# The second softmax's transposes in six of eight batches: 32x32 blocks on VectorE and 16 DMAs in place of TensorE's transposes

## The chip, the cores and the metric

The kernel runs on one core of one Trainium2 chip. The metric is the device time of one execution in microseconds (us). A profiled execution also has a span: the time from its first to its last recorded instruction.

## The reference

An attention of 8 batches between 512 tokens and 32 state rows per head (8 heads of 64), in both directions, feeds a dense feed-forward layer and a layer of 8 experts with one expert per token. The change touches the second direction only (`scores2`, `a2`, `sread`).

```
scores = scale * np.matmul(x, state.transpose(0, 1, 3, 2))
...
xread = np.matmul(a, state)
scores2 = scale * np.matmul(state, x.transpose(0, 1, 3, 2))
scores2 = scores2 - scores2.max(-1, keepdims=True)
a2 = np.exp(scores2)
a2 /= a2.sum(-1, keepdims=True) + 1e-09
sread = np.matmul(a2, x)
return np.concatenate([xread, sread], axis=2)
...
h = x @ w_in
g = h * np.clip(h + 3.0, 0.0, 6.0) / 6.0
x = g @ w_out
# then: logits, argmax over 8 experts, relu(x @ w1[e]) @ w2[e], two gates
```

## The kernel before

A batch's dense layer is a segment of 16 steps, one for each 128 of the 2048 hidden columns. In a step TensorE makes the hidden block `h` (`h_xread`, L470, 6 matmuls of 128x512), ScalarE and VectorE turn it into a high part `gh` and a low part `gl` (`act`, L499 to L502), and two steps later TensorE multiplies them into four output banks (`gemm2`, L509 to L511, 12 matmuls). So a step is 18 matmuls of equal shape.

In between stands the attention of the next batch, started by hand at numbered steps (`timetable`). `attn_rows` computes the scores once, with both softmaxes' inputs in two PSUM banks (tag `misc`); `columns` takes the exponentials for the second softmax into two tiles `e2` of 128x512. A row of such a tile is one state row of one head (four heads, 32 rows each), a column is a token. `cols_turn` (step 6) transposes them by TensorE in eight pieces of 128x128 into two `misc` banks (L378), and ScalarE copies them into two tiles `a2T` (L374), with tokens on the partitions. `cols_read` (step 7) multiplies `a2T` with the tokens `xq` in 32 small matmuls (L393, two passes each) and ScalarE scales the result (L399); `cols_x1` (step 8) transposes that result (L421) and keeps it in `x1h` and `x1l` for the last segment. `one_run` keeps the matmuls of such a part together and gives its first one every wait of the part.

Batch 0 and batch 1 are handled by a plan written out by hand (`plan`, `attn_cols`), batch 2 by `half_timetable`, batches 3 to 7 by `timetable`. Their `cols_turn` comes at 75, 128, 174, 210, 285, 361, 436 and 512 us in the profile.

The Tile scheduler orders each engine's instructions within what the program allows. Each engine then runs its list in order. All loads and most stores are issued by the SP queue, also in order; a DMA takes one of eight semaphores in turn, and the one that comes eight later waits until it has landed. The tag `x4` has four buffers of 512 KB: per batch two halves of the transposed tokens (`xT`) and two halves of the tokens (`xq`), and early on the raw weights and the two tiles `part`.

Of the kernel before, what the change touches and what calls it, by code (L numbers as in the profile page):

```python
# [8 lines left out]
F32 = mybir.dt.float32  # L9
# [4 lines left out]
ALU = mybir.AluOpType  # L14
# [4 lines left out]
NB, NH, NQ, NS, HD = 8, 8, 512, 32, 64  # L19
# [60 lines left out]
def tile_kernel(  # L80
# [16 lines left out]
    V, S, G, T, D = nc.vector, nc.scalar, nc.gpsimd, nc.tensor, nc.sync  # L97
# [3 lines left out]
    def pool(c, name, bufs=1, side=None, space=None):  # L101
        kw = {"space": space} if space else {}
        return c.enter_context(tc.tile_pool(name=name, bufs=bufs, side=side, reuse_waits="tile", **kw))
# [6 lines left out]
    ap = pool(actx, "ap", 2, side="right")  # L110
# [34 lines left out]
    def not_yet(i):  # L145

        tc.add_manual_dep(i.ins, marks[-1].name, LATER, reason="has time")
# [9 lines left out]
    st_t, aT, loads, e2_t, x_in, q_in = {}, {}, {}, {}, {}, {}  # L157
# [27 lines left out]
    def misc():  # L185
        users.append([])
        return psum("misc", 2), users[-1]

    def one_run(*parts):

        behind = [i for u in users[-2:] for i in u]
        built = [p() for p in parts]
        first = None
        for mms, needs, _ in built:
            behind += needs
        for mms, _, _ in built:
            for m in mms:
                i = m().ins
                if first is not None:
                    tc.add_manual_dep(i, first.name, LATER, reason="all at once")  # L200
                    continue
                first = i
                for d in behind:
                    tc.add_manual_dep(first, d.name, DEP, reason="banks are free and all operands are there")
        for b in built:
            b[2]()
# [139 lines left out]
    def columns(b, src, done=None):  # L346

        e2, sm = e2_t[b]
        mx, nm, s2, r2 = [sm[:, 2 * k:2 * k + 2] for k in range(4)]
        e2_t[b] = e2, s2, r2, []  # L350
        for e in range(2):
            i = V.tensor_reduce(mx[:, e:e + 1], src[e], axis=AX.X, op=ALU.max)
            if b < 2:
                not_yet(i)
            V.tensor_scalar(nm[:, e:e + 1], mx[:, e:e + 1], -0.125, None, op0=ALU.mult)
            j = S.activation(e2[e], src[e], AF.Exp, bias=nm[:, e:e + 1], scale=0.125, accum_out=s2[:, e:e + 1])
            e2_t[b][3].append(j.ins)
            if done:
                done[e] += [i.ins, j.ins]

    def cols_turn(b):

        e2, s2, r2, exps = e2_t.pop(b)
        V.tensor_scalar(s2, s2, 1e-9, None, op0=ALU.add)
        V.reciprocal(r2, s2)

        def part():
            made = [misc() for _ in range(2)]
            a2 = [ap.tile([128, 4, 128], F32, tag="wy", name="a2T", bufs=2) for _ in range(2)]

            def use():
                copies = []
                for e in range(2):
                    copies.append(S.copy(a2[e].rearrange("p a n -> p (a n)"), made[e][0]).ins)  # L374
                    made[e][1].append(copies[-1])
                e2_t[b] = a2, r2, copies

            return [lambda e=e, i=i: T.transpose(made[e][0][:, 128 * i:128 * i + 128],  # L378
                                                 e2[e][:, 128 * i:128 * i + 128], ident)
                    for e in range(2) for i in range(4)], exps, use  # L380

        return part

    def cols_read(b):

        def part():
            a2, r2, copies = e2_t[b]
            x_q = [loads.pop((b, k, "q")) for k in range(2)]
            psR, done = misc()

            def mm(e, i, j):
                h = 2 * j + e
                return T.matmul(psR[32 * j:32 * j + 32, HD * e:HD * e + HD], a2[e][:, i, 32 * j:32 * j + 32],  # L393
                                x_q[h // 4][:, i, HD * (h % 4):HD * (h % 4) + HD], start=(i == 0), stop=(i == 3),
                                tile_position=(0, 32 * j))

            def use():
                for e in range(2):
                    done.append(S.activation(a2[0][:, 0, HD * e:HD * e + HD], psR[:, HD * e:HD * e + HD], AF.Copy,  # L399
                                             scale=r2[:, e:e + 1]).ins)  # L400
                e2_t[b] = a2[0][:, 0, :], list(done)

            return [lambda e=e, i=i, j=j: mm(e, i, j) for e in range(2) for i in range(4) for j in range(4)], \
                [*copies, *q_in[b]], use

        return part

    def cols_x1(b):

        def part():  # L410
            read, reads = e2_t.pop(b)
            psX, done = misc()
            psX = psX[:, :128]

            def use():
                hi, lo = [x[:, :, NS * b:NS * b + NS] for x in (x1h, x1l)]
                src = psX.rearrange("p (j s) -> p j s", j=4)
                done.append(V.tensor_copy(hi, src).ins)
                done.append(V.tensor_tensor(lo, src, hi.bitcast(F32), op=ALU.subtract).ins)

            return [lambda: T.transpose(psX, read, ident)], reads, use  # L421

        return part

    def attn_cols(b):

        if b < 2:
            columns(b, e2_t[b][0])
            yield
        one_run(cols_turn(b))  # L430
        yield
        one_run(cols_read(b))
        yield
        one_run(cols_x1(b))
        yield
# [116 lines left out]
    def write_rows(r, c):  # L552

        xr = mp.tile([128, 8, 128], F32, tag="xr", name="xr", bufs=2)
        for k in range(4):
            i = V.transpose(xr[:, :, 32 * k:32 * k + 32], r.x2[k][:, 256 * c:256 * c + 256])
            for d in r.made[1::2]:
                tc.add_manual_dep(i.ins, d.name, LATER, reason="banks first")
        r0 = 128 * r.tile0 + 256 * c
        rows = xd[r0:r0 + 256, :].rearrange("(a u) (g n) -> g u a n", u=32, g=4)  # L560
        for g in range(4):
            D.dma_start(rows[g], xr[32 * g:32 * g + 32])

    def logits(r):

        def part():
            psl, done = misc()

            def mm(k):
                return T.matmul(psl[32 * k:32 * k + 32, :r.n], wg_sb[:, k, :], r.x2[k], start=True, stop=True,  # L570
                                tile_position=(0, 32 * k))

            def use():
                r.l4 = mp.tile([128, 512], F32, tag="r", name="l4")[:, :r.n]
                done.append(S.copy(r.l4, psl[:, :r.n]).ins)
                r.l4_made = done[-1]

            return [lambda k=k: mm(k) for k in range(4)], list(r.made), use

        return part  # L580
# [74 lines left out]
    def read_rows(r, c):  # L655

        nt = min(2, r.nt - 2 * c)
        r0 = 128 * r.tile0 + 256 * c
        t = mp.tile([128, 2, DM], F32, tag="xr", name="xt", bufs=2)[:, :nt, :]
        G.dma_start(t, xd[r0:r0 + 128 * nt, :].rearrange("(t p) n -> p t n", p=128))  # L660
        r.rows.extend(t[:, k, :] for k in range(nt))
# [538 lines left out]
    def timetable(b, r, att, shift):  # L1200

        rows = attn_rows(b) if att else iter(())
        todo = {}

        def at(k, *fs):
            todo.setdefault(k, []).extend(fs)

        at(2 + shift, lambda: write_rows(r, 0))
        at(3 + shift, lambda: write_rows(r, 1))
        at(5 + shift, lambda: read_rows(r, 0))  # L1210
        at(6 + shift, lambda: read_rows(r, 1))
        for k in range(4, 10):
            at(k, lambda: next(rows, None))
        if att:
            at(6, lambda: one_run(cols_turn(b)))
            at(7, lambda: one_run(cols_read(b), logits(r)))
            at(8, lambda: one_run(cols_x1(b), turn_logits(r)))
        else:
            at(6, lambda: one_run(logits(r)))
            at(7, lambda: one_run(turn_logits(r)))  # L1220
        at(9, lambda: choose(r))
        at(10, lambda: ranks(r))
        at(11, lambda: place(r), lambda: sort_rows(r, 0, 2))
        at(12, lambda: sort_rows(r, 2, 4, marks[-1:]))
        at(13, lambda: scatter(r, marks[-1:]))
        return todo
# [236 lines left out]
```

## Time and profile before

| | |
|---|---|
| time, median of 3 runs | 1101.79 us (1101.53 to 1102.30) |
| the profiled execution: time, span | 1100.96 us, 1099.2 us |
| TensorE busy, share of the span | 1073.2 us, 98% |
| VectorE, ScalarE, GpSimd busy | 65%, 50%, 11% |
| granted TensorE clock, mean | 0.999 of full speed |

The profiled execution took 1.8 us more than its span and 0.8 us less than the median. TensorE (PE in the rows) is busy almost all the time; PEld are its weight loads, which overlap its matmuls, DVE is VectorE, ACT is ScalarE, POOL is GpSimd, SPq is the issuing SP queue. A matmul's row lasts longer than its distance to the next, since matmuls are pipelined: distances between starts tell what a piece costs.

### The profile page before, as it was taken

The numbers are of one execution on the slowest core, as the hardware profiler recorded it, in microseconds if no ns is written. First come the engines' busy times: TensorE is split into PE (matmuls) and PEld (weight loads), VectorE is DVE, ScalarE is ACT, GpSimd is POOL, SyncE is SP. The second block draws the span as 40 slices with busy tenths as digits, with TensorE's granted clock in tenths as the row PEclk, the third lists the DMA queues.
The fourth block names the chain that finished last, engine by engine and source line by source line (L and its number), as shares of the span: only waits on it lengthen the run. The fifth ranks groups of instructions, "written<-read, shape, count | busy, mean of one in ns | idle before, by whom it ended". The sixth has DMA issues, their size and how long they took to land. (4 is left out here: it accounts for less than half of the span.)

```text
span 1099.2 us, 18698 instructions
## 1 busy us (share of the span) xinstructions
PE 1073.2 (98%) x6748; PEld 845.6 (77%) x6748; DVE 714.5 (65%) x1518; ACT 553.7 (50%) x1058; POOL 126.2 (11%) x138
## 2 busy tenths in 40 slices
PE   4999999999999999999999999999999999999997
PEld 1577777777777777777777899888869887988994
DVE  7988676755746747556554486986646655667761
ACT  4979644433433434334333344565545654566651
POOL 0000001230030030110300311220010010001001
PEclk9999999999999999999999999999999999999999
DMA  7657043613214114211130159676486679922500
GB/s 252 213 168 248 16 138 96 172 45 77 78 41 116 41 39 116 70 36 53 39 77 1 39 148 288 131 255 231 148 305 186 240 230 334 340 64 64 177 21 31
DMA packets 81251, 147.38 MB, mean 134 GB/s; under 512 B 13232, under 2 KB 49840, under 8 KB 81136
## 3 DMA queue, kind: packets, MB, share of 16 engines
q1 hardware_dynamic: 71776, 118.03, 34.7%
q0 software_dynamic: 9376, 28.09, 7.4%
q8 instruction: 55, 0.90, 0.4%
q14 instruction: 44, 0.36, 0.1%
HBM read 146.05 MB, written 29.68 MB: 160 GB/s over the span
## 5 line engine op out<-in xcount | busy, mean ns | idle before, releaser
L509 PE MATMUL o<-gh,wo 128*128 128x512 f32 x512 | 202.8, 396 | 0.0
L510 PE MATMUL o<-gh,wo 128*128 128x512 f32 x512 | 200.2, 391 | 0.2 <-DVE wo L782 0.2
L511 PE MATMUL o<-gl,wo 128*128 128x512 f32 x512 | 200.1, 391 | 0.0
L500 DVE SCALAR_TENSOR_TENSOR g<-r,h 128x512 f32<-128x512 f32 x128 | 87.3, 683 | 115.1 <-ACT r L499 114.6
L499 ACT ACTIVATE r<-h 128x512 f32<-128x512 f32 x128 | 76.4, 597 | 158.0 <-PE h L470 157.8
L1044 DVE TENSOR_TENSOR vl<-w2s,vh 128x512 fp32r<-128x512 f32 x128 | 87.8, 690 | 63.8 <-ACT vh L1043 56.2
L501 ACT CAST gh<-g 128x512 fp32r<-128x512 f32 x128 | 79.4, 620 | 82.2 <-DVE g L500 81.2
L1043 ACT CAST vh<-w2s 128x512 fp32r<-128x512 f32 x128 | 78.9, 621 | 78.7 <-PE o L1060 72.1
L502 DVE TENSOR_TENSOR gl<-g,gh 128x512 fp32r<-128x512 f32 x128 | 88.2, 689 | 44.7 <-ACT gh L501 39.3
L509 PEld LDWEIGHTS o<-gh,wo 128*128 128x128 f32 x512 | 96.1, 188 | 26.4 <-issue 6.1
L510 PEld LDWEIGHTS o<-gh,wo 128*128 128x128 f32 x512 | 96.2, 188 | 22.5 <-issue 1.5
L511 PEld LDWEIGHTS o<-gl,wo 128*128 128x128 f32 x512 | 96.1, 188 | 21.5 <-issue 1.0
L1034 DVE TENSOR_TENSOR wl<-w1s,wh 128x512 fp32r<-128x512 f32 x128 | 87.1, 688 | 35.2 <-ACT wh L1034 24.8
L1060 PE MATMUL o<-vh,hl 128*128 128x512 f32 x256 | 100.3, 392 | 0.9 <-DVE hl L1048 0.9
L1059 PE MATMUL o<-vl,hh 128*128 128x512 f32 x256 | 100.2, 392 | 0.0
L470 PE MATMUL h<-ah,sh 128*128 128x512 f32 x240 | 99.1, 414 | 0.9 <-ACT sh L453 0.7
L470 PE MATMUL h<-al,sh 128*128 128x512 f32 x240 | 94.7, 395 | 0.1
L470 PE MATMUL h<-ah,sl 128*128 128x512 f32 x240 | 93.8, 392 | 0.0
L1034 ACT CAST wh<-w1s 128x512 fp32r<-128x512 f32 x128 | 78.0, 621 | 29.5 <-PE h L1038 27.9
L1038 PEld LDWEIGHTS h<-xh,wh 128*128 128x128 f32 x512 | 76.9, 188 | 14.8 <-DVE hl L1048 2.4
L1038 PE MATMUL h<-xh,wh 128*128 128x256 f32 x512 | 82.1, 282 | 1.8 <-DVE hl L1048 1.8
L1056 PE MATMUL o<-vh,hh 128*128 128x512 f32 x256 | 81.2, 398 | 0.0
(234 smaller groups left out, 1770.8 us busy)
## 6 DMA issues: line engine op xcount, KB each, us to landing
w1s<-w SPq DMA_DIRECT2D x88, 512.0 KB
w2s<-w SPq DMA_DIRECT2D x88, 512.0 KB
xd<-xr SPq DMA_DIRECT2D x68, 128.0 KB
xt<-xd POOLq DMA_DIRECT2D x17, 512.0 KB
xT<-xT SPq DMA_DIRECT2D x16, 512.0 KB
wi<-w_in SPq DMA_DIRECT2D x16, 512.0 KB
wraw<-w_out SPq DMA_DIRECT2D x16, 512.0 KB
xq<-xq SPq DMA_DIRECT2D x16, 512.0 KB
```

The source lines that it names most:

```text
L470: T.matmul(ps, w[:, o:o + 128], a[:, e, :], start=(n == 0), stop=(n == 5))
L500: V.scalar_tensor_tensor(g6, r, 6.0, ps, op0=ALU.min, op1=ALU.mult)
L502: V.tensor_tensor(gl, g6, gh.bitcast(F32), op=ALU.subtract)
L509: T.matmul(po[k][:, :n], woh[ft][:, s], gh, start=first, stop=False)
L510: T.matmul(po[k][:, :n], wol[ft][:, s], gh, start=False, stop=False)
L511: T.matmul(po[k][:, :n], woh[ft][:, s], gl, start=False, stop=last)
L1034: last_w[:] = [S.copy(wh, a).ins, V.tensor_tensor(wl, a, wh.bitcast(F32), op=ALU.subtract).ins]
L1038: T.matmul(ps, w[:, k, :], x[:, k, :], start=(m == 0), stop=(m == 11))
L1044: V.tensor_tensor(vl, c, vh.bitcast(F32), op=ALU.subtract)
L1056: T.matmul(py[t], hh[:, sl], vh, start=(ft == 0), stop=False)
L1059: T.matmul(py[t], hh[:, sl], vl, start=False, stop=False)
L1060: T.matmul(py[t], hl[:, sl], vh, start=False, stop=(ft == 7))
```

## The change

For batch 1 and batches 3 to 7 the eight transposes by TensorE, their two `misc` banks and ScalarE's two copies go. `cols_move`, at step 5, lets VectorE transpose all 32x32 blocks of the two `e2` tiles into one tile `e2t` (two instructions), and the SP queue then moves the 4 x 4 groups of blocks to their partitions with 16 DMAs of 32 partitions x 1 KB, into one tile `a2T` for both halves. `cols_read` picks its weights from the new layout; its matmuls are the same in number and shape. `e2t` and `a2T` are in the tag `x4`. Batches 0 and 2 stay as they were.

```
+    moved = []
+
+    def cols_move(b):
+
+        e2, s2, r2, _ = e2_t.pop(b)
+        V.tensor_scalar(s2, s2, 1e-9, None, op0=ALU.add)
+        V.reciprocal(r2, s2)
+        two, a2T = [ap.tile([128, 4, 2, 128], F32, tag="x4", name=n, bufs=4) for n in ("e2t", "a2T")]
+        moves = []
+        for e in range(2):
+            V.transpose(two[:, :, e].rearrange("p g (c n) -> p c g n", n=32),
+                        e2[e].rearrange("p (c g q) -> p c g q", g=4, q=32))
+        for j in range(4):
+            for g in range(4):
+                moves.append(D.dma_start(a2T[32 * g:32 * g + 32, j].rearrange("p e x -> p (e x)"),
+                                         two[32 * j:32 * j + 32, g].rearrange("p e x -> p (e x)")).ins)
+        e2_t[b] = [a2T[:, :, e] for e in range(2)], r2, moves
+        moved.append(b)
+
     def cols_read(b):
 
         def part():
             a2, r2, copies = e2_t[b]
+
+            def w(e, i, j):
+                return a2[e][:, j, 32 * i:32 * i + 32] if b in moved else a2[e][:, i, 32 * j:32 * j + 32]
+
...
-                return T.matmul(psR[32 * j:32 * j + 32, HD * e:HD * e + HD], a2[e][:, i, 32 * j:32 * j + 32],
+                return T.matmul(psR[32 * j:32 * j + 32, HD * e:HD * e + HD], w(e, i, j),
...
     def attn_cols(b):
 
-        if b < 2:
-            columns(b, e2_t[b][0])
-            yield
-        one_run(cols_turn(b))
+        columns(b, e2_t[b][0])
+        if b:
+            cols_move(b)
+        yield
+        if not b:
+            one_run(cols_turn(b))
         yield
         one_run(cols_read(b))
         yield
...
         if att:
-            at(6, lambda: one_run(cols_turn(b)))
+            at(5, lambda: cols_move(b))
             at(7, lambda: one_run(cols_read(b), logits(r)))
             at(8, lambda: one_run(cols_x1(b), turn_logits(r)))
```

On TensorE, around the attention of batch 4 (285 to 292 us in the profile), the list before has the transposes behind the first matmul of a hidden block and `cols_read` 17 matmuls of 128x512 later (`o` are the output banks, `wo_510` the weights of a step, `xq_0_2732` the tokens of batch 4):

```order
L470 MATMUL h<-ah_2284,sh_1_0_2632 128x512
L378 MATMUL misc<-ident,e_2777 128x128 x4
L378 MATMUL misc<-ident,e_2778 128x128 x4
L470 MATMUL h<-al_2323,sh_1_0_2632 128x512
...
L510 MATMUL o_2668<-gh,wo_510 128x512
L511 MATMUL o_2668<-gl,wo_510 128x512
L393 MATMUL misc<-xq_0_2732,a2T 32x64 x2
L393 MATMUL misc<-xq_1_2734,a2T 32x64 x2
```

In the changed program the same place, from the matmul behind which `cols_read` stood (its line numbers from L384 on are higher: L495, L534 to L536, L416 are L470, L509 to L511, L393 of before):

```order
L536 MATMUL o_2680<-gl,wo_510 128x512
L495 MATMUL h<-ah_2296,sh_2_0_2849 128x512
L495 MATMUL h<-al_2335,sh_2_0_2849 128x512
L495 MATMUL h<-ah_2296,sl_2_0_2850 128x512
L495 MATMUL h<-ah_2296,sh_2_1_2851 128x512
L495 MATMUL h<-al_2335,sh_2_1_2851 128x512
L495 MATMUL h<-ah_2296,sl_2_1_2852 128x512
L534 MATMUL o_2677<-gh,wo_564 128x512
L535 MATMUL o_2677<-gh,wo_564 128x512
L536 MATMUL o_2677<-gl,wo_564 128x512
L534 MATMUL o_2678<-gh,wo_564 128x512
L535 MATMUL o_2678<-gh,wo_564 128x512
```

`cols_read` (L416) follows directly behind these rows: it moved 11 matmuls back. In batches 3 to 7 it is the same 11, in batch 1 it is 7. Its first matmul now waits for the semaphores of all 16 DMAs.

On VectorE, in the same stage, the list before reads (`bt` is the first softmax, `gl` and `sl` are low parts):

```order
L502 TENSOR_TENSOR gl<-g_2793,gh 128x512
L324 TENSOR_TENSOR bt<-bt,sm 128x1024
L364 TENSOR_SCALAR sm<-sm 128x2
L365 RECIPROCAL sm<-sm 128x2
L328 TENSOR_REDUCE sm<-bt 128x32
L454 TENSOR_TENSOR sl_2_0_2816<-misc,sh_2_0_2815 128x512
```

and in the changed program (L527 is L502 of before, L479 is L454):

```order
L527 TENSOR_TENSOR gl<-g_2805,gh 128x512
L389 TENSOR_SCALAR sm<-sm 128x2
L394 STREAM_TRANSPOSE e2t<-e_2789 128x4x4x32
L390 RECIPROCAL sm<-sm 128x2
L394 STREAM_TRANSPOSE e2t<-e_2790 128x4x4x32
L324 TENSOR_TENSOR bt<-bt,sm 128x1024
L479 TENSOR_TENSOR sl_2_0_2850<-misc,sh_2_0_2849 128x512
```

The two transposes and the two short operations stand directly behind the `gl` of the step, ahead of the first softmax's subtraction (L324).

On the SP queue, behind the eight stores of the batch before (`xd`, L587, L562 before), the list of the changed program reads:

```order
L161 DMA st_2693<-sts 128x128
L587 DMA xd<-xr 32x8x128 x8
L398 DMA a2T<-e2t 32x256 x16
L170 DMA xT_0_3399<-xT 128x1024
L170 DMA xT_1_3401<-xT 128x1024
L179 DMA xq_0_3448<-xq 128x1024
```

The 16 moves (L398) are new; the rest has its order of before. In batch 1 they stand behind the last raw weights, and the two loads of `part` (L1156 before), which stood between the raw weights, now come behind the moves.

## Rows read from the trace of the kernel before

**Rows 1.** The page: TensorE's busy time, and GB/s in 40 slices of the span.
```profile
PE 1073.2 (98%) x6748; PEld 845.6 (77%) x6748; DVE 714.5 (65%) x1518; ACT 553.7 (50%) x1058; POOL 126.2 (11%) x138
...
GB/s 252 213 168 248 16 138 96 172 45 77 78 41 116 41 39 116 70 36 53 39 77 1 39 148 288 131 255 231 148 305 186 240 230 334 340 64 64 177 21 31
```
**Rows 2.** Windows: busy us of PE, PEld, DVE, ACT, POOL; PEclk, DMA share, GB/s.
```profile
275.00:300.00 25.00, 25.00 (x196) 18.64 (x189) 19.74 (x40) 12.15 (x24) 0.00 (x0) 1.00 0.25 85
```
**Rows 3.** Timeline of PE at three turns: start us, duration us, what, [idle before].
```profile
127.94 0.39 PE L511 MATMUL o<-gl,wo 128*128 128x512 f32 x1
...
129.28 0.40 PE L470 MATMUL h<-al,sh 128*128 128x512 f32 x1
...
208.81 0.39 PE L470 MATMUL h<-ah,sh 128*128 128x512 f32 x1
209.52 1.09 PE L378 MATMUL misc<-ident,e 128*128 128x128 f32 x8 [0.32 <-DVE sl L454]
...
210.68 0.40 PE L470 MATMUL h<-ah,sl 128*128 128x512 f32 x1
...
284.64 0.39 PE L511 MATMUL o<-gl,wo 128*128 128x512 f32 x1
284.87 0.39 PE L470 MATMUL h<-ah,sh 128*128 128x512 f32 x1
...
286.31 0.40 PE L470 MATMUL h<-ah,sl 128*128 128x512 f32 x1
```
**Rows 4.** Timeline of PE where batches 1, 3 and 4 are read.
```profile
133.27 1.10 PE L393 MATMUL misc<-xq,a2T 128*32 128x64 f32 x64
...
214.44 1.10 PE L393 MATMUL misc<-xq,a2T 128*32 128x64 f32 x64
...
290.07 1.10 PE L393 MATMUL misc<-xq,a2T 128*32 128x64 f32 x64
```
**Rows 5.** Groups by line and shape: count | busy us, mean ns of one | idle before.
```profile
L336 DVE STREAM_TRANSPOSE af<-bt 128x1024 f32<-128x1024 f32 x7 | 8.7, 1238 | 0.0
...
L378 PE MATMUL misc<-ident,e 128*128 128x128 f32 x56 | 7.5, 277 | 0.3 <-DVE sl L454 0.3
...
L556 DVE STREAM_TRANSPOSE xr<-x2T 128x256 f32<-128x256 f32 x36 | 13.6, 414 | 4.4 <-issue 4.4
...
L365 DVE RECIPROCAL sm<-sm 128x2 f32<-128x2 f32 x8 | 1.3, 165 | 0.2
```
**Rows 6.** Timeline of DVE in batches 1, 3 and 4.
```profile
124.94 0.17 DVE L364 TENSOR_SCALAR sm<-sm 128x2 f32<-128x2 f32 x1 [0.88 <-ACT e L356]
...
204.70 1.22 DVE L324 TENSOR_TENSOR bt<-bt,sm 128x1024 f32<-128x1024 f32 x1
...
280.33 1.22 DVE L324 TENSOR_TENSOR bt<-bt,sm 128x1024 f32<-128x1024 f32 x1
...
287.34 0.69 DVE L502 TENSOR_TENSOR gl<-g,gh 128x512 fp32r<-128x512 f32 x1
```
**Rows 7.** Timeline of the SP queue's issues; xN from the first's start to the last's end.
```profile
302.15 0.33 SPq L161 DMA_DIRECT2D st<-sts  x1
...
338.54 1.85 SPq L562 DMA_DIRECT2D xd<-xr  x4
...
756.15 4.54 SPq L925 DMA_DIRECT2D xg<-xs  x8
```
**Rows 8.** Windows behind the load of `st` (64 KB) at 302.15.
```profile
303.00:303.50 0.50, 0.50 (x4) 0.42 (x3) 0.50 (x2) 0.19 (x1) 0.00 (x0) 1.00 0.38 113
303.50:304.00 0.50, 0.50 (x4) 0.41 (x3) 0.50 (x1) 0.35 (x1) 0.00 (x0) 1.00 0.07 18
```
**Rows 9.** Timeline of POOL behind the four stores of `xd` at 338.54.
```profile
343.02 0.75 POOL L660 DMA_DIRECT2D xt<-xd  x1 [20.84 <-DMA xd<-xr]
```
**Rows 10.** Timeline of PE: batch 2's scores, and the first use of a `gl`.
```profile
152.30 1.09 PE L226 MATMUL misc<-xT,st 64*32 64x512 f32 x16
...
293.91 0.39 PE L511 MATMUL o<-gl,wo 128*128 128x512 f32 x1
```

## The prediction

> **What bounds the kernel now.** I read the page first, then windows around the turned batches, then the timelines of TensorE, VectorE and SP there. TensorE is busy 98% of the span [rows 1], and in the 25 us around batch 4's second softmax all 25.00, at the full clock (1.00 of 2.4 GHz), while VectorE has 5 us to spare [rows 2]. So a piece of TensorE work that goes comes back in full, unless TensorE then waits for something; nothing that VectorE or ScalarE do there counts until TensorE waits for it. The chain of waits says little here: in this trace it reaches back only over the last microseconds. What decides is one wait: the first matmul of `cols_read` needs all 16 moves landed, and everything TensorE has left stands behind it.
>
> **What goes.** The price of a turn is the distance between the matmul ahead of it and the second one behind it (the first behind it is late too), less two plain distances. A plain one is 284.87 - 284.64 = 0.23 us. Batch 4: 286.31 - 284.87 - 0.46 = 0.98 us. Batch 3: 210.68 - 208.81 - 0.46 = 1.41; there the turn also waited for a `misc` bank that VectorE had not released. Batch 1: 129.28 - 127.94 - 0.46 = 0.88 [rows 3]. Batches 5 to 7 repeat batch 4. Sum: 0.88 + 1.41 + 4 x 0.98 = 6.2 us. Two PSUM copies by ScalarE per batch go too; I count them at nothing, since ScalarE is busy only 12 of 25 us [rows 2].
>
> The group row of these transposes shows 277 ns as the mean of one [rows 5], but eight of them cost 0.98 us, because they overlap [rows 3]. The Trainium skill, "TensorE: Matmul & The Clock Gate", Part 4: PE-mode transpose, gives about 275 ns for one in a kernel's context: its figure is the row's duration, and taken eight times one after the other in six batches it would make 13.2 us. The distances between starts decide, and they say 6.2.
>
> **What is added on VectorE.** Two transposes of 128x512 from SBUF to SBUF. The nearest row is a 128x1024 at 1238 ns, 0.62 us for half of it; the other bound is twice a 128x256, 0.83 us, a row with a scattered output [rows 5]. I take 0.65. With the two short operations (0.165 each, only moved ahead [rows 5]) the block lasts 1.63 us (1.57 to 2.0). In the new order it starts where L324 started: at 280.33 in batch 4, 204.70 in batch 3 [rows 6]. So `e2t` is ready at 281.96 and 206.33. In batch 1 the first transpose fits into the 0.88 us in which VectorE waited for the exponential, the second comes behind the short operation at 124.94 [rows 6]: ready at 124.94 + 0.17 + 0.65 = 125.76. What is behind it on VectorE comes up to 1.3 us later. The cover: the `gl` written from 287.34 to 288.03 is first read at 293.91 [rows 6, 10], 5.9 us later (I paired them by their order), so this costs nothing; without the cover it would cost up to 1.3 us in each batch, 8 in all.
>
> **What is added on SP.** 16 issues in a row, then the landing of the last. Call the time from `e2t` to the last landing T = 15 x pace + landing. Pace: one issue of 128 rows lasts 0.33 us; four stores of 256 pieces take 1.85, 0.46 each; eight loads of 32 KB with register work between them take 4.54, 0.57 each [rows 7]. Ours have 32 rows each and one wait, no register work: I take 0.40, between the first two. Landing: the small load issued at 302.15 moved bytes until at most 304.0 [rows 7, 8], 1.85 us; the reader of four stores started at 343.02 [rows 9], 3.1 us after the fourth issue (338.54 + 3 x 0.46). I take 2.0, near the first, because these 32 KB stay in SBUF and the stores went to HBM. T = 8.0 us; bounds 15 x 0.33 + 1.85 = 6.8 and 15 x 0.57 + 3.1 = 11.65. The semaphore of eight issues earlier costs nothing in this range: eight issues last 2.6 us or more, longer than a landing of 2.0.
>
> **Against when it is needed.** `cols_read` of batch 4 started at 290.07 [rows 4]. Now it stands 11 matmuls later (11 x 0.228 = 2.5), and the turn ahead of it is gone (0.98): 291.6. That is 9.6 us after `e2t`; batches 5 to 7 the same. Batch 3: 214.44 + 2.5 - 1.41 = 215.5, 9.2 after. Batch 1: 7 matmuls, 133.27 + 1.6 - 0.88 = 134.0, 8.2 after. With T = 8.0 no batch waits; batch 1 has 0.2 us left, so I allow 0.1 for it.
>
> **What else moves.** Behind the moves on SP stand the next batch's `xT` and `xq`, which now also wait for buffers that `cols_read` and `cols_x1` free; they are wanted only a batch later, 290.07 - 214.44 = 75.6 us [rows 4]. In batch 1 the two `part` and batch 2's two `xT`, 2 MB, now start behind its `cols_read`, at about 135; batch 2's scores want the `xT` at 152.30 [rows 10]. In 17 us that is 123 GB/s; the same kind of loads ran at 252 in the first slice [rows 1], so they take some 8 us plus 2 to land. If they didn't fit, the loss would be a few us once. GpSimd's queue is not touched. The 3 MB moved inside SBUF meet little: the DMA share there is 0.25 [rows 2].
>
> **Sum.** -6.2 + 0.1 = -6.1 us. The profiled execution is 1100.96, so 1094.9; the median stands 0.8 above it: 1101.79 - 6.1 = 1095.7 us.
>
> **The rivals.**
> *Part of it is eaten.* T lies between 8.7 and 10.2 us: batch 1 waits T - 8.2, batch 3 T - 9.2, four batches T - 9.6 each. T = 9.7 gives 1.5 + 0.5 + 0.4 = 2.4, so 1098.0. For it: the stores' pace of 0.46 with a landing of 2.5 makes 9.4 [rows 7, 9]. Against: those have eight times as many pieces.
> *Slower: the issues hold up TensorE.* The sum of the waits passes 6.2 us when 6 T - 55.8 = 6.2, at T = 10.3, a pace of 0.55 with a landing of 2.0. At the upper bound of 11.65 the waits are 3.45 + 2.45 + 4 x 2.05 = 14.1 and the time 1101.79 - 6.2 + 14.1 = 1109.7. For it: the eight small loads came at 0.57 [rows 7]. Against: those have register work between the issues.
> *Slower by far: each move pays its whole landing before the next.* Then T = 16 x 1.85 = 29.6, the waits 6 x 29.6 - 55.8 = 122, the time near 1217. Against it: four stores were issued within 1.85 us and their reader started 4.5 us after the first issue [rows 7, 9], where one after the other they would need 7.4. The Trainium skill, "DMA: Bandwidth & Descriptors", Rules for kernel authors, advises to merge many small transfers and says that those under 64 KB pay mostly overhead; the rows show that overhead here as latency that overlaps, not as a sum.
> *No change: what TensorE gives back is lost later,* to a transfer in the expert stage that does not come earlier with it. Against: those transfers wait for buffers that TensorE's own progress frees. It would give 1101.8.
>
> **How the numbers follow.** The forecast, all six turns back and at most 0.5 us of waits: 62 in 100. Partly eaten: 17. Slower by the issues: 10; by the whole landing: 1. No change: 10. A measurement of this kernel can tell about 0.2%, 2.2 us, from no change. Faster by more than that means below 1099.6: the forecast and most of the second case (waits below 4.0), 62 + 14 = 76. Within: 3 + 10 = 13, and of the slower case what lies below 1104, 3, together 16. Slower: 8. The forecast's own range is 1094.9 to 1096.6 (the spread of the runs, 0.4 each way, and 0.5 of waits). The range reaches up over the second case: 1094.8 to 1100.2, which holds 62 + 17 = 79.
>
> **What would show it.** Right: no rows of TensorE's transposes in six batches; `cols_read` of batch 4 near 290 to 292 on the new time line with no idle time ahead of it; two rows of VectorE of 0.6 to 0.7 us; 16 issues of SP within 6 to 7 us; the later stages each about 6 us earlier. Wrong: idle time of TensorE ahead of `cols_read`, released by the moves. The number falls with the pace on SP above all: 0.15 us more per issue is 2.25 us more in T, and from T = 9.6 on each further microsecond costs six.

## The result and the profile after

The changed kernel takes 1114.10 us, median of five runs (1112.07 to 1117.83); the kernel before, in the same comparison, 1101.79. The ratio is 1.0117, with a 95% interval of 1.0096 to 1.0138: 1.2% slower. The prediction said 1095.7 and a range up to 1100.2. The profiled execution took 1112.34 us, its span is 1110.5, and its mean granted clock is 0.996, where before it was 0.999. Two of the six runs of the experiment through HBM took 1337.88 and 2543.55 us, in a slower state, and are left out of its figures.

The page, TensorE's busy time and the others' (before: [rows 1]):

```profile
PE 1071.7 (97%) x6700; PEld 843.3 (76%) x6700; DVE 719.3 (65%) x1530; ACT 548.5 (49%) x1046; POOL 126.5 (11%) x138
```

TensorE has less work and a longer span, so it waits more. The timeline of PE shows where: each of the six `cols_read` (L416), with the idle time directly ahead in brackets, and in batches 1 and 4 the matmul ahead of it (before: [rows 4], no idle time there).

```profile
135.05 0.39 PE L534 MATMUL o<-gh,wo 128*128 128x512 f32 x1
138.97 1.10 PE L416 MATMUL misc<-xq,a2T 128*32 128x64 f32 x64 [3.53 <-issue]
...
223.15 1.05 PE L416 MATMUL misc<-xq,a2T 128*32 128x64 f32 x61 [2.12 <-DMA a2T<-e2t]
...
297.44 0.39 PE L535 MATMUL o<-gh,wo 128*128 128x512 f32 x1
299.80 1.46 PE L416 MATMUL misc<-xq,a2T 128*32 128x64 f32 x64 [1.97 <-issue]
...
377.64 0.55 PE L416 MATMUL misc<-xq,a2T 128*32 128x64 f32 x25 [1.58 <-DMA a2T<-e2t]
...
454.54 0.66 PE L416 MATMUL misc<-xq,a2T 128*32 128x64 f32 x33 [2.25 <-DMA a2T<-e2t]
...
530.98 0.72 PE L416 MATMUL misc<-xq,a2T 128*32 128x64 f32 x37 [1.80 <-DMA a2T<-e2t]
```

Together 13.25 us. Two of the six are named "issue" (nothing that the profile shows); the view of the moves' line, L398, puts all six, 13.3 us, down to them. Its first line below gives the shortest, median and longest duration of an issue in ns:

```profile
L398 SPq DMA_DIRECT2D a2T<-e2t x96: 512/589/998, 127.2 to 528.8; - x96
...
  PE misc L416: 13.3, 6
```

The timeline of DVE: the second transpose of batch 1, and the whole block of batch 4 (`e2t` is ready when the second transpose ends). Then the timeline of SP's issues in batches 1, 3 and 4 (before: [rows 6, 7]):

```profile
126.47 0.70 DVE L394 STREAM_TRANSPOSE e2t<-e 128x512 f32<-128x512 f32 x1
...
286.53 0.16 DVE L389 TENSOR_SCALAR sm<-sm 128x2 f32<-128x2 f32 x1
286.63 0.71 DVE L394 STREAM_TRANSPOSE e2t<-e 128x512 f32<-128x512 f32 x1
...
287.31 0.69 DVE L394 STREAM_TRANSPOSE e2t<-e 128x512 f32<-128x512 f32 x1
```

```profile
127.20 10.06 SPq L398 DMA_DIRECT2D a2T<-e2t  x16
...
211.23 10.43 SPq L398 DMA_DIRECT2D a2T<-e2t  x16
...
288.07 10.02 SPq L398 DMA_DIRECT2D a2T<-e2t  x16
```

In batch 4 `e2t` is ready at 288.00, the first issue follows at 288.07, the last one ends at 298.09, and `cols_read` starts 1.71 us after that. The pace is (10.02 - 0.59) / 15 = 0.63 us. So T, from `e2t` to the start of `cols_read`, is 11.8 us. TensorE was ready at 297.83 (297.44 + 0.39), 9.8 us after `e2t`: the wait is the difference. In the other five batches the traces give the same picture: T is 11.4 to 12.0 us, and TensorE was ready 8.3 us after `e2t` in batch 1 and 9.5 to 9.9 in the others.

One thing more is in the windows behind the waits (columns as in [rows 2]; the third number from the right is PEclk):

```profile
138.00:142.00 4.00, 3.03 (x70) 2.47 (x70) 0.00 (x1) 0.52 (x2) 0.00 (x0) 0.74 0.49 159
142.00:146.00 4.00, 4.00 (x17) 3.24 (x16) 0.58 (x2) 0.06 (x1) 0.00 (x0) 0.83 0.78 247
298.00:302.00 4.00, 2.20 (x72) 1.46 (x72) 0.47 (x1) 0.52 (x2) 0.00 (x0) 0.80 0.29 92
302.00:306.00 4.00, 4.00 (x22) 2.65 (x15) 1.32 (x4) 1.71 (x3) 0.00 (x0) 0.78 0.85 268
376.00:380.00 4.00, 2.42 (x75) 1.50 (x75) 0.69 (x1) 0.80 (x3) 0.00 (x0) 1.00 0.37 99
```

Behind the waits of batches 1 and 4 the granted clock fell to its lower level for a part of 8 us. I estimate what that cost by the missing share of each window: 4 x (0.26 + 0.17) = 1.7 us, and 4 x (0.20 + 0.22) = 1.7. Behind that of batch 5 it stayed at 1.00, as it did behind those of batches 3, 6 and 7.

Now the account closes. Equal matmuls of both traces tell how late the changed program is at a place. Here are the blocks of L226 that stand behind batch 1's `cols_read`, ahead of batch 3's, and behind those of batches 3 to 7:

```profile
157.92 1.09 PE L226 MATMUL misc<-xT,st 64*32 64x512 f32 x16
...
203.71 1.09 PE L226 MATMUL misc<-xT,st 64*32 64x512 f32 x16
...
231.56 1.09 PE L226 MATMUL misc<-win,st 64*32 64x512 f32 x16
...
335.70 1.09 PE L226 MATMUL misc<-win,st 64*32 64x512 f32 x16
...
411.92 1.09 PE L226 MATMUL misc<-win,st 64*32 64x512 f32 x16
...
498.35 1.09 PE L226 MATMUL misc<-win,st 64*32 64x512 f32 x16
...
565.25 1.09 PE L226 MATMUL misc<-win,st 64*32 64x512 f32 x16
```

In the trace of before the same blocks start at 152.30, 198.23, 225.33, 326.85, 402.46, 487.62 and 553.67. So the program is late by 5.62, 5.48, 6.23, 8.85, 9.46, 10.73 and 11.58 us at these places; ahead of batch 1 it was late by 1.44.

| batch | turn gone (as predicted) | wait | clock | sum | shift in the trace |
|---|---|---|---|---|---|
| 1 | -0.88 | 3.53 | 1.7 | +4.4 | +4.18 |
| 3 | -1.41 | 2.12 | 0 | +0.7 | +0.75 |
| 4 | -0.98 | 1.97 | 1.7 | +2.7 | +2.62 |
| 5 | -0.98 | 1.58 | 0 | +0.6 | +0.61 |
| 6 | -0.98 | 2.25 | 0 | +1.3 | +1.27 |
| 7 | -0.98 | 1.80 | 0 | +0.8 | +0.85 |

The six make +10.3 of the span's +11.3. The 1.44 ahead of batch 1 arose almost whole in the first 30 us, where all engines and the SP queue run the same list in both traces; the same place is late by 0.7 to 2.2 us in the profiles of all the experiments below, whether they are faster or slower. So it doesn't come from the moves or the waits; what makes it is not known.

### The profile page after: what moved, and what is told of

It reads as the page before. It is cut to its first block, busy times and chain, and to the rows that moved or that the text cites. A ratio compares the mean times of both kernels' runs of the same rounds, so it can differ in the third digit from the quotient of the medians.

```text
span 1110.5 us, 18738 instructions
## 1 busy us (share of the span) xinstructions
PE 1071.7 (97%) x6700; PEld 843.3 (76%) x6700; DVE 719.3 (65%) x1530; ACT 548.5 (49%) x1046; POOL 126.5 (11%) x138
## 5 line engine op out<-in xcount | busy, mean ns | idle before, releaser
L534 PE MATMUL o<-gh,wo 128*128 128x512 f32 x512 | 203.3, 397 | 0.0
L536 PE MATMUL o<-gl,wo 128*128 128x512 f32 x512 | 201.6, 394 | 0.0
L536 PEld LDWEIGHTS o<-gl,wo 128*128 128x128 f32 x512 | 96.7, 189 | 26.4 <-issue 6.3
L534 PEld LDWEIGHTS o<-gh,wo 128*128 128x128 f32 x512 | 96.6, 189 | 26.3 <-issue 6.1
L527 DVE TENSOR_TENSOR gl<-g,gh 128x512 fp32r<-128x512 f32 x128 | 87.8, 687 | 41.2 <-ACT gh L526 34.1
L495 PE MATMUL h<-ah,sh 128*128 128x512 f32 x240 | 98.2, 410 | 0.9 <-ACT sh L478 0.7
L495 PE MATMUL h<-al,sh 128*128 128x512 f32 x240 | 94.2, 392 | 0.1
L495 PE MATMUL h<-ah,sl 128*128 128x512 f32 x240 | 93.7, 391 | 0.0
```

The lines of the kernel that those rows point to most:

```text
L495: T.matmul(ps, w[:, o:o + 128], a[:, e, :], start=(n == 0), stop=(n == 5))
L527: V.tensor_tensor(gl, g6, gh.bitcast(F32), op=ALU.subtract)
L534: T.matmul(po[k][:, :n], woh[ft][:, s], gh, start=first, stop=False)
L536: T.matmul(po[k][:, :n], woh[ft][:, s], gl, start=False, stop=last)
```

## The experiments

**The theory:** an issue of a move inside SBUF costs SP 0.63 us whatever it carries, so T is 15 x 0.63 + 2.2 = 11.7 us, more than TensorE has until `cols_read`; the rest follows from that. **Rivals:** the landing or the bytes set T; the added work on VectorE or the traffic costs time; the missing turns gave nothing back. One more rival, that an issue waits until the move eight issues earlier has landed, can be settled from the changed kernel's own trace: none of SP's waits at L398 is for a landing, and the pace is 0.63 among the first eight issues as among the last eight. The scheduler places `cols_read` by what it is told of the moves, so it stands at another place in some variants; the expectations count that.

**Without the moves.** In `cols_move` the loop of DMAs goes, and `cols_read` takes the blocks as VectorE left them.

```
-        two, a2T = [ap.tile([128, 4, 2, 128], F32, tag="x4", name=n, bufs=4) for n in ("e2t", "a2T")]
+        two = a2T = ap.tile([128, 4, 2, 128], F32, tag="x4", name="e2t", bufs=4)
...
-                moves.append(D.dma_start(...))
```

> The changed kernel without the 16 moves: cols_read multiplies the blocks where VectorE's transposes left them, so the second softmax's result is not the reference's. Theory (issues on SP): everything that was lost came from the moves; cols_read stands 11 matmuls earlier, as in the kernel before, and waits for nothing; the gain of removing the turns is seen alone: 6.2 us, about 1095.6 us (1094.9 to 1096.6). Rival (the loss comes from VectorE's transposes or from the missing turns themselves): above 1101, with TensorE waiting for VectorE.

Measured: 1095.2 us, ratio 0.9937 (0.9924 to 0.995), mean clock 0.998, no idle time ahead of `cols_read`. The removed turns are worth 6.9 us (5.5 to 8.4). The trace agrees: by the same blocks of L226 the six batches give back 0.98, 1.46, 1.03, 1.04, 1.03 and 1.01 us, 6.55 together, so VectorE's transposes cost nothing there. All that was lost came with the moves.

**`cols_read` later.** All 16 moves stay. Batches 3 to 7 are edited as below; in batch 1 the hand-written plan calls the same parts later.

```
-            at(7, lambda: one_run(cols_read(b), logits(r)))
-            at(8, lambda: one_run(cols_x1(b), turn_logits(r)))
+            at(7, lambda: one_run(logits(r)))
+            at(8, lambda: one_run(turn_logits(r)))
+            at(9, lambda: one_run(cols_read(b)))
+            at(10, lambda: one_run(cols_x1(b)))
```

> The changed kernel with cols_read two steps later (9 in place of 7) in batches 3 to 7 and some 29 matmuls later in batch 1; it computes the whole reference. Theory (issues on SP): 16 issues 0.63 us apart and a landing of 2.1 make 11.7 us from e2t to the last landing, as in the changed kernel, but cols_read now stands 25 plain matmuls (5.7 us) further back, 29 (6.6 us) in batch 1, more than the 1.6 to 3.5 us that TensorE waited. So no idle time ahead of cols_read, no half clock in the middle of the program, and the gain of 6.2 us comes through: about 1095.6 us (1094.9 to 1096.6). Rival (the loss is contention, or work that VectorE does): the moves and the transposes are all still there, so 1108 or more, with idle time somewhere else.

Measured: 1098.02 us, ratio 0.9961 (0.9948 to 0.9974), clock 0.999, no idle time ahead of any `cols_read`. The same moves with the same pace, and the kernel is faster than before: the loss was the wait, with the clock behind it, and not the traffic. But the median is 2.4 us above what the theory said.

**The company of `cols_read`.** First with the turn of the logits in its block (the edit is shown against the run before):

```
-            at(8, lambda: one_run(turn_logits(r)))
-            at(9, lambda: one_run(cols_read(b)))
+            at(9, lambda: one_run(cols_read(b), turn_logits(r)))
```

> As later2, but the batch's cols_read shares its block with the small matmuls that turn the logits (step 9), so that TensorE's run of 128x512 matmuls is broken as often as in the changed kernel. In later2 nothing waited, yet each of the batches 3 to 7 gave back 0.3 us less than without the moves; a block of other matmuls costs about 0.1 us on each side (0.32 to 0.33 from start to start in place of 0.23), and later2 has two blocks more per batch. Theory (breaks): later3 gives back what the kernel without moves gives, 0.98 to 1.0 in each of batches 4 to 7 and about 1.1 to 1.4 in batch 3: 1095.5 to 1096.5 us. Rival (standing later itself costs, by what waits behind cols_read): no better than later2, 1098.0.

Measured: 1097.14 us, ratio 0.9954 (0.994 to 0.9969), and in its trace each of batches 4 to 7 gives back about 0.75 us, 0.05 more than later2. Fewer breaks were not what was missing. Two blocks of L226 on either side of batch 5's `cols_read` show it; in the trace of before they start at 326.85 and 402.46, 75.61 us apart, and here 74.84:

```profile
325.37 1.09 PE L226 MATMUL misc<-win,st 64*32 64x512 f32 x16
...
400.21 1.09 PE L226 MATMUL misc<-win,st 64*32 64x512 f32 x16
```

Then with the blocks as the changed kernel has them, two steps later (the edit is shown against the changed kernel; batch 1 is moved as before):

```
-            at(7, lambda: one_run(cols_read(b), logits(r)))
-            at(8, lambda: one_run(cols_x1(b), turn_logits(r)))
+            at(9, lambda: one_run(cols_read(b), logits(r)))
+            at(10, lambda: one_run(cols_x1(b), turn_logits(r)))
...
-        at(9, lambda: choose(r))
-        at(10, lambda: ranks(r))
+        at(10 if att else 9, lambda: choose(r))
+        at(11 if att else 10, lambda: ranks(r))
```

> As later3, but cols_read keeps its block with the logits and cols_x1 its block with their turn, as in the changed kernel, both two steps later (9 and 10), and the routing's choice and ranks one step later; the whole reference. In later3 TensorE lost about 0.28 us per batch against the kernel without moves: its three blocks of small matmuls cost 1.09, 1.54 and 0.17 us there, 1.98, 0.47 and 0.07 without moves. Theory (the company of cols_read in its block): later4 gives back 0.98 to 1.0 us in each of batches 4 to 7 and 1.4 in batch 3: about 1.3 us below later3, 1095.4 to 1096. Rival (standing later costs, whatever the block): as later3, 1097.1, or more if the routing comes too late for the scatter.

Measured: 1095.66 us, ratio 0.9952 (0.9938 to 0.9966), clock 0.998. In the times later4 stands 1.5 us below later3, but the two ran on different chips, each beside its own runs of before (1101.15 and 1102.05), and their ratios are almost the same (0.9952 and 0.9954); so the times don't show a gain of the blocks. The traces do. The same two blocks are 74.57 us apart here, 0.27 less than in later3:

```profile
324.55 1.09 PE L226 MATMUL misc<-win,st 64*32 64x512 f32 x16
...
399.12 1.09 PE L226 MATMUL misc<-win,st 64*32 64x512 f32 x16
```

Batches 4 to 7 give back 1.01 to 1.04 us each and batch 3 gives 1.47, as much as without the moves. So standing later costs nothing by itself, and the regrouped blocks, with the logits and the routing moved along, are worth about 0.3 us a batch; why one order of small matmuls is dearer than another stays open. Later4 computes the reference and its median is 5.5 us under that of the kernel before. Its batch 4, SP's issues and then PE:

```profile
280.59 10.02 SPq L398 DMA_DIRECT2D a2T<-e2t  x16
```

```profile
295.62 0.39 PE L536 MATMUL o<-gl,wo 128*128 128x512 f32 x1
295.94 1.10 PE L416 MATMUL misc<-xq,a2T 128*32 128x64 f32 x64
```

Ten microseconds of issues as in the changed kernel, and `cols_read` follows a plain matmul at 0.32 us with nothing idle.

**What an issue costs, by its form.** `cols_read` takes the blocks as they are, so nothing waits for a move, and the result is not the reference's; each batch issues another form (`hop` is scratch in HBM; batch 5, not shown, has 4 moves of `a2T[:, j]` from `two[:, j]`).

```
+                if b == 1:
+                    D.dma_start(hop[j, g], src)
+                elif b == 3:
+                    D.dma_start(dst, hop[j, g])
+                elif b == 4:
+                    D.dma_start(dst, src)
+                elif b == 6:
+                    D.dma_start(dst[:, 0, :64], src[:, 0, :64])
+                elif b == 7:
+                    D.dma_start(dst[:8], src[:8])
```

> What does one issue cost, by its form? The blocks are read where VectorE's transposes left them, so nothing waits for a move and the second softmax's result is not the reference's; the moves are there, but of another form in each batch: 1: 16 of 32 rows x 1 KB from SBUF to HBM; 3: the same from HBM to SBUF; 4: the same inside SBUF, as in the changed kernel; 5: 4 of 128 x 1 KB inside SBUF; 6: 16 of 32 x 256 B; 7: 16 of 8 x 1 KB inside SBUF. If the cost of an issue is one of every move inside SBUF: 0.63 in batches 4 to 7, 0.40 to 0.50 in 1 and 3. If it is one of moves of few rows: 0.63 in 1, 3, 4, 6 and 0.40 in 5. If by bytes: 6 and 7 fall to a third. The time: nothing waits, so 1095.4, unless the moves' traffic itself costs something.

The groups by line: number of issues, and the shortest, median and longest in ns; L404 is batch 1, then 3, 4, 5, 6, 7 in order.

```profile
L404 SPq DMA_DIRECT2D hop<-e2t x16: 338/419/1796, 127.8 to 136.1; - x16
```

```profile
L406 SPq DMA_DIRECT2D a2T<-hop x16: 302/420/422, 201.1 to 209.8; - x16
```

```profile
L408 SPq DMA_DIRECT2D a2T<-e2t x16: 572/589/1500, 282.0 to 292.4; - x16
```

```profile
L399 SPq DMA_DIRECT2D a2T<-e2t x4: 533/599/649, 356.5 to 358.5; - x4
```

```profile
L410 SPq DMA_DIRECT2D a2T<-e2t x16: 561/589/1142, 430.5 to 440.0; - x16
```

```profile
L412 SPq DMA_DIRECT2D a2T<-e2t x16: 624/624/739, 505.7 to 515.9; - x16
```

To or from HBM an issue of 32 rows takes 0.42 us. Inside SBUF it takes 0.59 to 0.62 with 8 rows or 128, with 8 KB or 128 KB. About 0.04 us lie between two issues that follow each other directly. That is the first case of the expectation: these issues cost the same whatever they carry. Sixteen issues to or from HBM were hardly shorter all the same, 8.7 and 9.1 us in place of 10: one issue of batch 1 lasted 1.80 us, and in batch 3 SP waited 2.1 us for earlier moves to land. The time was 1096.82 us in the one run, with the moves' traffic there and nobody waiting for it.

**The same with the wait.** 16 moves of 128 rows x 256 B, in place of the changed kernel's; the result is not the reference's:

```
+                c = slice(64 * (g % 2), 64 * (g % 2) + 64)
+                moves.append(D.dma_start(a2T[:, j, g // 2, c], two[:, j, g // 2, c]).ins)
```

> The changed kernel with 16 moves of the same 32 KB each, but 128 rows of 256 B in place of 32 rows of 1 KB, from the same partition to the same partition, so the blocks are not put in place and the result is not the reference's. Is the issue's 0.59 us that of 32 rows, or of any move inside SBUF? cols_read stands 3 matmuls earlier than in the changed kernel (4 in batch 1). If 128 rows are issued at 0.40 to 0.46, as loads and stores of before: 15 x 0.43 + 2.1 = 8.6 us from e2t, due after 8.9 (8.5 in batch 3, 7.3 in batch 1): about 1.4 us of waits and 1097. If every such move takes 0.63: 11.7 us, waits of 2.8 four times, 3.2 and 4.4, together 18.8 and 1114.4, and more with each fall of the clock.

Measured: 1118.67 us in one run, clock 0.992. SP in batch 4:

```profile
291.09 10.13 SPq L399 DMA_DIRECT2D a2T<-e2t  x16
```

10.13 us for 16 issues, as with 32 rows. The six waits, 2.0 to 3.6 us each, make 15.7 us, where 18.8 were expected. The clock fell behind four of them (batches 1, 3, 4 and 7). An estimate from these figures, with 1.7 us for each fall, gives 1102.0 - 6.2 + 15.7 + 4 x 1.7 = 1118.3.

**Twice as many issues, the same bytes.** In place of the changed kernel's one move:

```
+                for e in range(2):
+                    moves.append(D.dma_start(a2T[32 * g:32 * g + 32, j, e], two[32 * j:32 * j + 32, g, e]).ins)
```

> The changed kernel with each move cut in two: 32 of 32 rows x 512 B, the whole reference. Theory (count of issues): 31 x 0.63 + 2.2 = 21.7 us from e2t; cols_read stands 25 matmuls later than in the changed kernel (31 in batch 1) and is due after 15.5: waits of 6.2 us in each of six batches, 37 together, so 1133 plus about 1.7 for each fall of the clock to half behind a stall, 1135 to 1144. Rival (bytes decide): a pace of 0.31, 11.8 us, no waits, 1095.4.

Measured: 1158.49 us in one run, clock 0.974. Batch 4, SP's issues, PE's wait, and the windows behind it:

```profile
300.53 20.14 SPq L399 DMA_DIRECT2D a2T<-e2t  x32
```

```profile
322.31 1.93 PE L416 MATMUL misc<-xq,a2T 128*32 128x64 f32 x64 [5.70 <-DMA a2T<-e2t]
```

```profile
322.00:326.00 4.00, 3.64 (x72) 1.94 (x72) 0.00 (x0) 0.52 (x2) 0.00 (x0) 0.50 0.53 169
326.00:330.00 4.00, 3.17 (x9) 2.42 (x10) 2.42 (x6) 2.19 (x4) 0.00 (x0) 0.50 0.89 313
330.00:334.00 4.00, 4.00 (x28) 2.09 (x27) 3.59 (x12) 2.35 (x5) 0.00 (x0) 0.88 0.17 62
```

The issues take twice the time, so the count decides. The waits (5.6 to 7.3 us) make 37.6 us, as expected. The time is 15 to 23 us above what was expected, and that is the clock: behind a wait of 5.7 us it stays at 0.50 for some 9 us. Over the whole span the mean clock is 0.974 in place of 0.999, and 0.025 x 1156.7 = 29 us, an estimate of the work lost, part of it while TensorE waited anyway. I had counted 1.7 us for each wait, from waits of 2 to 3.5 us.

**Two queues.** Every second move is issued by ScalarE's queue.

```
-                moves.append(D.dma_start(
+                moves.append((D, S)[g % 2].dma_start(
...
```

> The changed kernel with every second move issued by ScalarE's queue: eight by SP, eight by ScalarE; the whole reference. Theory (each queue issues at its own pace): 7 x 0.63 + 2.2 = 6.6 us from e2t to the last landing; cols_read stands 11 matmuls earlier than in the changed kernel and is due 7.3 us after e2t (6.7 in batch 1): no waits for moves and about 1095.4 us, if ScalarE can spare the 5 us of eight issues; what it does behind them (casts of sh, relu of h) comes up to 5 us later, and TensorE then waits at those in place of the moves, up to 3 us a batch. Rival (one limit for all moves inside SBUF, whatever the queue): 11.7 us from e2t, waits of 4.4 us in five batches and 5 in batch 1, together 27: 1122, and more with each fall of the clock.

Measured: 1100.41 us, ratio 0.9979 (0.997 to 0.9988). SP, ACT and PE in batch 4, and PE in batch 3:

```profile
284.92 5.27 SPq L398 DMA_DIRECT2D a2T<-e2t  x8
```

```profile
284.88 5.01 ACTq L398 DMA_DIRECT2D a2T<-e2t  x8
289.93 1.07 ACT L478 CAST sh<-misc 128x512 fp32r<-128x512 f32 x2 [6.86 <-DMA a2T<-e2t]
```

```profile
292.11 1.10 PE L416 MATMUL misc<-xq,a2T 128*32 128x64 f32 x64
```

```profile
215.94 1.10 PE L416 MATMUL misc<-xq,a2T 128*32 128x64 f32 x64 [2.03 <-DVE sl L479]
```

In batches 4 to 7 each queue keeps its own pace, 0.63 to 0.67 us, side by side with the other, and `cols_read` waits for nothing (0.06 us at most) although it stands as early as in the kernel before. Batch 1 waited 1.0 us. Batch 3 waited 2.03, which the profile puts down to VectorE's `sl`; that follows ScalarE's `sh`, which stood behind ScalarE's eight issues. A fall of the clock came behind it. These eight issues took 7.04 us and not 5.01: in their middle SP's waits show 2.0 us for an earlier move to land, and ScalarE's queue paused at the same time. So the rival of one common limit falls for the pace of the issues. The price that the theory named for ScalarE is there in batch 3, but a late landing, which the theory had not named, made it 2 us longer.

The Trainium skill, "DMA: Bandwidth & Descriptors", Rules for kernel authors, says that spreading transfers over several queues saves only issue time and wins no bandwidth. The trace agrees on issue time, 5.3 us in place of 10.0 in batch 4, and issue time was what bound here; no run here tests bandwidth.

**Through HBM and back.** Five issues in place of the loop of 16.

```
+        i = D.dma_start(hop[b], two).ins
+        for j in range(4):
+            moves.append(D.dma_start(a2T[:, j], hop[b, 32 * j:32 * j + 32].rearrange("q g e x -> g q e x")).ins)
```

> The changed kernel with the 16 moves replaced by five issues: one store of e2t to HBM (128 rows of 4 KB) and four loads back (128 rows of 1 KB), each of which puts a row group in place; it computes the whole reference and carries twice the bytes. Theory (the number and form of the issues decides, not the bytes): 0.4 for the store's issue, 2.2 to land, 3 more issues of 0.42 and 2.2 to land make about 6.2 us from e2t to the last landing; cols_read, 11 matmuls earlier than in the changed kernel, is due 7.1 us after e2t (6.7 in batch 3, 6.6 in batch 1), so no waits and about 1095.6 us. With landings of 3.1 us, 8.0: waits of 0.9 four times, 1.3 and 1.4, together 6.3, so 1101.9. Rival (landing or bytes decide): two landings and twice the bytes make it worse than the changed kernel's waits, above 1108.

Measured: 1134.98 us, median of four runs, ratio 1.0298 (1.0283 to 1.0313), clock 0.986. Batch 5, SP and PE, then the same in batch 7, behind which no next batch's loads stand:

```profile
377.77 0.34 SPq L397 DMA_DIRECT2D hop<-e2t  x1
380.43 2.21 SPq L399 DMA_DIRECT2D a2T<-hop  x4
382.69 8.96 SPq L171 DMA_DIRECT2D xT<-xT  x2
```

```profile
389.35 0.92 PE L416 MATMUL misc<-xq,a2T 128*32 128x64 f32 x25 [4.23 <-DMA a2T<-hop]
```

```profile
542.12 2.21 SPq L399 DMA_DIRECT2D a2T<-hop  x4
```

```profile
550.25 1.10 PE L416 MATMUL misc<-xq,a2T 128*32 128x64 f32 x64 [3.65 <-DMA a2T<-hop]
```

The expectation of the theory missed, and the rival (landing or bytes decide) came true. In batch 5 the store landed within 2.7 us, little more than counted. The four loads' issues, whose rows are regrouped on the way, took 0.51 to 0.53 us each, where I had put 0.42. But `cols_read` started 7.2 us after the start of the last of them, where I had put 2.2. The next batch's `xT`, issued right behind them in batch 5, is not the reason: in batch 7 nothing stands behind them, and it is still 6.4 us (550.25 - 543.82). There the DMA engines moved the 512 KB at 76 to 98 GB/s for most of that time, with nothing else on it. So few issues alone do not make a short T: the transfer of these loads, in pieces of 1 KB, set when they landed. T was 11.0 to 11.8 us in five batches, hardly other than with the 16 moves, and 15.1 in batch 3, where the loads were issued only 6.4 us behind the store; the waits, 29.0 us together, are longer because `cols_read` stands 11 matmuls earlier here.

## Why the prediction was wrong

**The step that failed is the pace in "What is added on SP".** I took 0.40 us, between a load's single issue and a store's row, with a bound of 0.57 from loads with register work [rows 7]. It measured 0.63 in the changed kernel, above even that bound. All the rows that I had were of transfers to or from HBM; with the move's own 32 rows those take 0.46 from start to start where nothing is waited for, and inside SBUF it is 0.17 more. Fifteen paces made T 3.4 us longer than I took, and with a landing of 2.3 it was 11.8 in place of 8.0. So "no batch waits" turned into six waits, 13.25 us together, against 6.2 gained.

**The landing was right:** 2.0 predicted; 2.30 from the start of the last issue in batch 4 (299.80 - 297.50), and 1.9 to 2.3 over the six batches.

**When it is needed was right:** 9.6 us after `e2t` predicted, 9.8 in batch 4; 8.2 in batch 1, 8.3 measured (135.05 + 0.39 less 126.47 + 0.70). In batch 3 it was 9.9, where 9.2 was predicted.

**VectorE was right:** a transpose takes 0.70 (0.65 predicted), the block 1.47 us (1.63). `e2t` is ready at 288.00; predicted 281.96 plus the 6.2 us by which the program is late there. Its cover held: without the moves no batch lost anything to VectorE, as what they give back shows.

**The gain was right:** 6.2 predicted; without the moves 6.9 (5.5 to 8.4) measured in the times and 6.55 in the trace, with 1.01 to 1.04 us in batches 4 to 7 (0.98 predicted), 1.46 in batch 3 (1.41) and 0.98 in batch 1 (0.88). Batch 2's loads behind batch 1's moves fitted in, as predicted.

**The rival "slower: the issues hold up TensorE" is what happened**, with its own formula: at its upper bound of 11.65 us it gave waits of 14.1 us; 13.25 came. That its T is so close to the measured 11.8 is luck: its pace of 0.57 was 0.06 too low and its landing of 3.1 was 0.8 too high, which cancel over 15 paces. I gave it 10 in 100 on the ground that the loads at 0.57 had register work between them. That ground did not hold: a move inside SBUF costs more than they did, without any. And its time of 1109.7 was still too low for the 1114.1, since it held the waits and not the clock (3.4 us in the profiled execution).

**The clock was missing from the sum.** A wait of TensorE in a kernel that is busy 98% of the time costs itself and, in this kernel, sometimes a stretch at the lower clock behind it: 1.7 us each in two of six batches of the profiled execution. The other runs' mean clocks lie between 0.992 (the run of 1117.83 us) and 0.996, so they probably had more such stretches; their traces were not taken.

**The range was too narrow for the same reason:** the bound of the unknown cost was taken from rows of another kind of transfer, and six waits hang on it at once.

## What to carry to other kernels

A chain of small DMAs that somebody waits for cost its count times the queue's pace here; take that pace from a row with the same source and destination memory, and where there is none, measure it before counting on a margin of a sixth (8.0 us against 9.6). A move that is issued at the same time but read two steps later was free here: the gain of taking work from TensorE comes only if its reader stands far enough behind. Fewer issues are no cure by themselves: the five through HBM took as long as the sixteen. And a wait of a nearly always busy TensorE is to be priced with the clock behind it: here nothing or about 1.7 us behind waits of 1.6 to 3.7 us, and more behind those of 5.6 to 7.3.

## What was not expected of the hardware

An issue of a DMA inside SBUF took 0.59 to 0.62 us with 8 to 128 rows and 8 to 128 KB, one to or from HBM of the same 32 rows 0.42. The memory is not all that sets the price, since loads from HBM with regrouped rows took 0.51; what else does was not separated. Two queues issued such moves side by side, each at its own pace (four of six batches). The granted clock fell behind a wait of 1.97 us (batch 4) and not behind those of 2.12 and 2.25 (batches 3 and 6), nor behind one of 3.65 (batch 7 of the run through HBM), so the length of the wait alone does not tell; what else decides stays open.
